# Six store tiles, weight loads on another queue, and K rows in a shared tile, in the first stage of a two-part kernel

## The chip, the cores and the metric

The kernel runs on one core of a Trainium2 chip. The metric is the device time of one execution in microseconds (us), lower is better. The kernels ran on the same chip beside runs of the kernel before.

## The reference

Two independent parts, whose outputs are put side by side. Part A is a long convolution (a Hyena-like block): a four-tap shift of `k`, a product with `v`, a convolution over 2048 steps by FFT, and a product with `q`. Part B is attention with a recurrent memory: 64 segments of 32 rows, each of which needs the memory rows that the segment before it produced.

```python
# part A, S = 2048, D = 1024
k_shift = sum(k_pad[:, t:t + S] * shift_k[:, 3 - t] for t in range(4))
kv = k_shift * v
y  = irfft(rfft(kv, 2 * S) * rfft(ssm_k, 2 * S))[:S] + kv * ssm_D
a  = q * y
# part B, 64 segments, 8 memory rows, 32 heads of 128
for s in range(64):
    h = concatenate([mem, x[:, 32 * s:32 * s + 32]])
    q, k, v = (einsum('btd,dhe->bhte', h, W) for W in (Wq, Wk, Wv))
    p = softmax(where(mask, q @ k.T * scale, -1e9))
    o = einsum('bhte,hed->btd', p @ v, Wo)
    mem = o[:, :8]; outs.append(o[:, 8:])
return concatenate([a, b], axis=-1)      # everything in bfloat16
```

## The kernel before

The work runs in this order: a prologue; stage 1 of the FFT over 16 units of rows (this is what the change edits); a dense projection with the first K weights (tiles `kb_ps`), whose start I call the **hand-over**; the later FFT stages with more projections; and then the attention loop of 64 segments, which streams weights through a ring called `wring`. The parts that the change touches:

```python
X_LOAD, K_LOAD = 4, 0
...
k0pool = tc.tile_pool(name="a1_k0", bufs=4)              # row pairs of k, 4 KB each
wk     = tc.tile_pool(name="a1_wk", bufs=3)
ints   = slot16([128, 4096], I32, "ints")                # integers of the sine tables
shflat = slot16([1, 4096], BF, "shflat")                 # the taps; takes the OTHER 16 KB tile
nc.sync.dma_start(shflat[:], shift_k...)
...
def stage1(u_tile, t, scratch):
    sb = wk.tile([128, 2, 1024], BF, tag="s1_sb")         # three store tiles (bufs=3 of the pool)
    for h in range(2):
        pt = ps_big.tile([128, 1024], F32, tag="big")
        for hf in range(2):
            nc.tensor.matmul(pt[:, hf*512:(hf+1)*512], lhsT=F1h[h], rhs=u_tile[:, hf*512:(hf+1)*512])
        nc.scalar.copy(sb[:, h, :], pt[:])                # ScalarE empties PSUM
    return nc.sync.dma_start(scratch...[t], sb[:])        # 512 KB to DRAM

for t in range(16):
    ...                                                   # 8 transposes of ssm_k -> kt
    stage1(kt, t, SK1)
    if t % 2 == 0:
        K0 = k0pool.tile([128, 2048], BF, tag="K0")
        nc.sync.dma_start(K0[:], pair_rows(k, t))
        Vp = io.tile([128, 2048], BF, tag="Vt")           # two buffers
        nc.gpsimd.dma_start(Vp[:], pair_rows(v, t))
    u = wk.tile([128, 1024], BF, tag="u", bufs=2)
    ...                                                   # 8 products on VectorE (tile prod, bufs=8),
                                                          # summed on PE into ks_ps; u = ks_ps * Vt
    su_stores.append(stage1(u, t, SU1))
    if tables: tables.pop(0)()                            # sine tables for later stages
stage1_done(su_stores)

def stage1_done(su):
    make_consts(); make_xbt(su)                           # x rows, transposed: XBT (PE, then ScalarE)
    for kc in range(8):
        with tc.issue_after(su[K_LOAD + kc]):             # behind that store, on the sync queue
            group(0, 0, which=[kc], ws=ws)                # load a K weight into slot pw0..pw7;
    dense(0, 0, ws)                                       # if streamed later: also copy it to DRAM (WS), on GpSimd
```

`slot16` alternates between two 16 KB tiles, stage0 and stage1; `slot4` is here a function that alternates between two 4 KB slots (`pair`).

## Time and profile before

| | |
|---|---|
| three runs of the kernel before | 2158.19 us median (2157.98 to 2163.79) |
| span of its profile, mean granted clock of TensorE | 2160.2 us, 0.978 |
| hand-over | 117.75 us |
| first matmul of the attention loop | 429.0 us |
| end of the first and of the 64th segment | 462.2 and 2147.4 us |

I take the end of a segment from the start of ScalarE's last cast of that segment's output, and call the stretch between these two ends the loop. Two more things are needed later. First, the page's list of transfers, with the KB of one transfer and the median us from issue to landing, in the kernel before:

```profile
SK<-s_sb SPq DMA_DIRECT2D x16, 512.0 KB, 5.0
SU<-s_sb SPq DMA_DIRECT2D x16, 512.0 KB, 5.1
```

These are the stores out of the three tiles. Second, busy time by stretch in the loop (stretch, its length, then PE, PEld, DVE, ACT, POOL with counts, clock, DMA share, GB/s):

```profile
462.20:2147.38 1685.18, 1363.66 (x33447) 776.11 (x33451) 613.32 (x2205) 433.33 (x819) 295.59 (x938) 0.99 1.01 387
```

The DMA share of 1.01 suggests that its transfers bound the loop, at 387 GB/s; PE is busy for 1364 of 1685 us, and its longest wait there, 108.8 us in 258 pieces, is for `wring`. Nothing in the change is inside this stretch.

### The profile page before, as it was taken

What the parts mean: (1) busy time and instruction counts of PE and PEld (TensorE: products, weight loads), DVE (VectorE), ACT (ScalarE), POOL (GpSimd) and SP (SyncE); (2) the same over time, 40 slices, a digit from 0 to 9 for tenths busy, and PEclk for the clock granted to TensorE, in tenths of its full rate; (3) what the DMA queues carried; (4) which work ended last, traced back from release to release, by engine and by line L of the source; (5) the groups of instructions that cost most, each with busy time, mean ns of one, the idle gap of its engine ahead of it and who ended that gap; (6) DMA issues with size and microseconds to landing.
All of it is one profiled execution on the core that took longest, in us unless ns stands there. A gap on an engine that the chain in (4) does not pass through costs nothing. (4 is left out here: it accounts for less than half of the span.)

```text
span 2160.2 us, 81529 instructions
## 1 busy us (share of the span) xinstructions
PE 1745.9 (81%) x35731; PEld 939.3 (43%) x35764; DVE 866.7 (40%) x2735; ACT 638.5 (30%) x1131; POOL 426.5 (20%) x1100
## 2 busy tenths in 40 slices
PE   6887988978878877888888878888877888878886
PEld 3432333434444444444444444444444444444444
DVE  9726852133333333333333333333333333333332
ACT  6845521222222222222222222222222222222222
POOL 3013432201111111111112111111111111111111
PEclk9998999989999999999999999999999999999999
DMA  9888989999999999999999999999999999999996
GB/s 322 315 334 298 296 311 378 313 371 386 392 378 392 387 377 379 391 392 394 392 393 395 390 388 384 391 381 383 390 389 375 389 392 384 394 394 392 393 391 269
DMA packets 238311, 802.29 MB, mean 371 GB/s; under 512 B 34721, under 2 KB 34753, under 8 KB 237953
## 3 DMA queue, kind: packets, MB, share of 16 engines
q1 hardware_dynamic: 207186, 728.20, 88.0%
q0 software_dynamic: 25552, 58.39, 7.8%
q10 hardware_dynamic: 5216, 10.49, 1.3%
q8 instruction: 279, 4.57, 0.9%
q14 instruction: 78, 0.64, 0.1%
HBM read 737.56 MB, written 62.39 MB: 370 GB/s over the span
## 5 line engine op out<-in xcount | busy, mean ns | idle before, releaser
L920 PEld LDWEIGHTS <-rec 128*32 128x32 bf16 x12351 | 318.6, 96 | 470.9 <-issue 249.1
L920 PE MATMUL acc<-wring,rec 128*32 128x512 bf16 x3765 | 371.4, 384 | 132.4 <-DMA wring<-WS 114.9
L929 ACT CAST qkv_sb<-acc 128x512 bf16<-128x512 f32 x384 | 225.1, 586 | 650.1 <-PE acc L920 646.6
L1006 PEld LDWEIGHTS <-OT 128*32 128x32 bf16 x8192 | 220.2, 97 | 181.3 <-issue 153.6
L1006 PE MATMUL yacc<-wring,OT 128*32 128x256 bf16 x3072 | 156.6, 279 | 95.5 <-DMA wring<-WS 57.7
L920 PE MATMUL acc<-Wmid,rec 128*32 128x512 bf16 x3072 | 225.9, 384 | 0.0
L920 PE MATMUL acc<-Wres,rec 128*32 128x512 bf16 x2816 | 221.2, 380 | 0.0
L866 PEld LDWEIGHTS <-OTB 128*16 128x16 bf16 x4096 | 106.2, 90 | 101.3 <-issue 92.4
L992 ACT CAST OT<-OTp 128x512 bf16<-128x512 f32 x128 | 75.0, 586 | 241.7 <-PE OTp L984 241.7
L1022 DVE COPY KT<-tps 128x512 bf16<-128x512 bf16 x64 | 27.2, 425 | 295.3 <-PE tps L935 295.3
L993 DVE CAST OTB<-OTp 128x128 bf16<-128x128 f32 x128 | 37.4, 292 | 261.2 <-ACT OT L992 261.2
L821 POOL DMA_DIRECT2D rec<-REC x64 | 37.5, 586 | 520.9 <-issue 264.0
L768 DVE TENSOR_SCALAR wring<-OTp 128x384 int32<-128x384 int32 x126 | 112.3, 891 | 53.8 <-PE acc L920 45.7
L920 PE MATMUL acc<-pw,rec 128*32 128x512 bf16 x1544 | 131.1, 382 | 0.0
L896 POOL COPY KT<-rec 128x128 bf16<-128x128 bf16 x128 | 38.8, 303 | 419.8 <-PE SB L944 398.2
L881 POOL DMA_DIRECT2D out_dram<-YB x128 | 73.3, 580 | 242.2 <-DVE YB L879 221.8
L950 DVE TENSOR_REDUCE mx<-SB 128x5 f32<-128x200 f32 x128 | 47.1, 368 | 179.8 <-PE SB L944 179.8
L935 PEld LDWEIGHTS <-qkv_sb 128*128 128x128 bf16 x1024 | 62.9, 97 | 105.1 <-ACT qkv_sb L929 61.6
L866 PE MATMUL SB<-wring,OTB 128*16 128x256 bf16 x1488 | 79.6, 276 | 35.6 <-DVE SB L845 29.6
L935 PE MATMUL tps<-ident,qkv_sb 128*128 128x128 bf16 x1024 | 101.2, 221 | 8.0
L1006 PE MATMUL yacc<-Wlate,OT 128*32 128x256 bf16 x2048 | 105.3, 276 | 2.4 <-issue 1.7
L1062 ACT CAST Y<-yacc 128x256 bf16<-128x256 f32 x64 | 23.8, 372 | 243.8 <-PE yacc L1006 239.2
(231 smaller groups left out, 2688.4 us busy)
## 6 DMA issues: line engine op xcount, KB each, us to landing
wring<-WS SPq DMA_DIRECT2D x1215, 512.0 KB, 7.3
rec<-REC POOLq DMA_DIRECT2D x64, 192.0 KB, 6.1
SK<-s_sb SPq DMA_DIRECT2D x16, 512.0 KB, 5.0
SU<-s_sb SPq DMA_DIRECT2D x16, 512.0 KB, 5.1
Kg<-SK SPq DMA_DIRECT2D x32, 256.0 KB, 5.2
Ug<-SU SPq DMA_DIRECT2D x32, 256.0 KB, 5.8
REC<-stage POOLq DMA_DIRECT2D x16, 512.0 KB, 11.2
zt<-SZ SPq DMA_DIRECT2D x16, 512.0 KB, 7.6
```

The source lines that it names most:

```text
L768: nc.vector.tensor_scalar(out=dst, in0=src, scalar1=0, scalar2=None, op0=ALU.bitwise_or)
L821: nc.gpsimd.dma_start(rec[:], REC[:, s, :])
L866: nc.tensor.matmul(self.acc[32 * dq:32 * dq + W, x - o:y - o], lhsT=self.OTB[:, c, 4 * g + i, :], rhs=r, start=first and not self.seeded, ...
L881: nc.gpsimd.dma_start(bass.AP(outb.tensor, outb.offset + (SEG * NB * self.b + NX) * 2048 + 256 * dq, [[2048 * SEG, NB], [2048, 8], [1, 256 ...
L896: nc.gpsimd.tensor_copy(KT[:, :, :, 32:40], KBs[:, 128 * g:128 * g + 128].rearrange("p (c i t) -> p i c t", c=4, i=4))
L920: nc.tensor.matmul(self.acc[32 * c:32 * c + 32, x - 512 * c:y - 512 * c], lhsT=hT[:, kc, :], rhs=r, start=(kc == 0 and x == 512 * c), stop ...
L929: nc.scalar.copy(sb[:], self.acc[:])
L935: nc.tensor.transpose(tp[:, i * 128:(i + 1) * 128], sb[:, i * 128:(i + 1) * 128], ident[:])
L950: nc.vector.tensor_reduce(out=mx[:], in_=S, op=ALU.max, axis=AX.X)
L992: nc.scalar.copy(OT[:], o_view[:, :, :, 0:32])
L993: nc.vector.tensor_copy(OTB[:, :, 4 * g:4 * g + 4, 8 * j:8 * j + 8], o_view[:, :, :, 32:40])
L1006: nc.tensor.matmul(yacc[32 * dq:32 * dq + 32, x - o:y - o], lhsT=OT[:, c, i, :], rhs=r, start=(h == 0 and x == o), stop=(h == 31), tile_po ...
```

## The change

Its intent: ScalarE waits in stage 1 for one of three store tiles (8.5 us in the profile before). The row pairs of `k` move into a 16 KB tile that is otherwise idle, which frees room for six store tiles. For that tile to be free, the tap rows and the tables' scratch move into weight slots that are still empty. And the first K weights leave the sync queue, to be issued by GpSimd behind the `v` rows. The core of the diff (cut: the body and signature of `group`, the matmul that reads the tap rows, the handing on of the list `v_loads`, and the same edit in a second table function):

```diff
-X_LOAD, K_LOAD = 4, 0
+X_LOAD, K_LOAD = 4, 2
-        k0pool = c1.enter_context(tc.tile_pool(name="a1_k0", bufs=4, side="right"))
-        shflat = slot16([1, 4096], BF, "shflat")
-        nc.sync.dma_start(shflat[:], shift_k.rearrange("(o d) j -> o (d j)", o=1))
+        shflat = [slot4(i)[0:1, :] for i in (6, 7)]
+        for i in range(2):
+            nc.sync.dma_start(shflat[i], shift_k.rearrange("(o d) j -> o (d j)", o=1)[:, 2048 * i:2048 * i + 2048])
-            sines = slot4()[:, 0:32 * NP].rearrange("p (a b) -> p a b", b=32)
+            sines = slot4(4 + x)[:, 0:32 * NP].rearrange("p (a b) -> p a b", b=32)
-            sb = wk.tile([128, 2, 1024], BF, tag="s1_sb", name="s1_sb")
+            sb = wk.tile([128, 2, 1024], BF, tag="s1_sb", bufs=6, name="s1_sb")
+        kring = slot16([128, 4, 2048], BF, "K0")
-                K0 = k0pool.tile([128, 2048], BF, tag="K0", name="K0")
-                nc.sync.dma_start(K0[:], pair_rows(k, t))
+                K0 = kring[:, t // 2 % 4, :]
+                nc.sync.dma_start(K0, pair_rows(k, t))
-                nc.gpsimd.dma_start(Vp[:], pair_rows(v, t))
+                v_loads.append(nc.gpsimd.dma_start(Vp[:], pair_rows(v, t)))
-            u = wk.tile([128, 1024], BF, tag="u", bufs=2, name="u")
+            u = wk.tile([128, 1024], BF, tag="u", bufs=3, name="u")
-                    pr = wk.tile([128, 512], BF, tag="prod", bufs=8, name="prod")
+                    pr = wk.tile([128, 512], BF, tag="prod", bufs=10, name="prod")
-            with tc.issue_after(su[K_LOAD + kc].ins):
-                group(0, 0, which=[kc], ws=ws)
+            with tc.issue_after(vl[K_LOAD + kc // 2].ins):
+                group(0, 0, which=[kc], ws=ws, eng=nc.gpsimd)
-    run_a(ps0, pair, slot16, stage1_done, fill)
+    run_a(ps0, pw, slot16, stage1_done, fill)
```

More of the change, by code (lines that the diff above doesn't have):

```diff
@@ L171, in a_kernel @@
                 nc.tensor.matmul(pt[:, e * 512:(e + 1) * 512], lhsT=ones_row[0:1, :],
-                                 rhs=shflat[0:1, hf * 1024 + e * 512:hf * 1024 + (e + 1) * 512], start=True, stop=True)
+                                 rhs=shflat[hf // 2][:, hf % 2 * 1024 + e * 512:hf % 2 * 1024 + (e + 1) * 512], start=True, stop=True)
             nc.scalar.copy(SH[:, :, hf * 256:(hf + 1) * 256], pt[:].rearrange("p (d j) -> p j d", j=4))
@@ L214, in table_n @@
             nc.vector.tensor_scalar(out=aN, in0=aN, scalar1=4095, scalar2=None, op0=ALU.bitwise_and)
-            sines = slot4()[:, 0:64 * NS].rearrange("p (a b) -> p a b", b=64)
+            sines = slot4(4 + y)[:, 0:64 * NS].rearrange("p (a b) -> p a b", b=64)
             act_sin(sines, aN, 12)
@@ L237, in a_kernel @@
         nc.sync.dma_start(Kx[113:128], kx_src[112:127])
-        su_stores = []
+        su_stores, v_loads = [], []
+        kring = slot16([128, 4, 2048], BF, "K0")
         ktiles = {c: Kx[:, c + 3, :] for c in (-3, -2, -1)}
@@ L271, in a_kernel @@
                 tables.pop(0)()
-    stage1_done(su_stores)
+    stage1_done(su_stores, v_loads)
     def valid_re(k1):
@@ L491, in b_kernel, with stage1_done @@
     pools = {}
-    def stage1_done(su):
+    def stage1_done(su, vl):
         make_consts()
@@ L551, in b_kernel, with group @@
     copied, got = [], []
-    def group(m, g, temps={}, which=range(8), ws=None):
+    def group(m, g, temps={}, which=range(8), ws=None, eng=nc.sync):
         ws = ws or [None] * 8
@@ L557, in group @@
             if ch in res:
-                got.append(nc.sync.dma_start(res[ch], dram_chunk(ch)))
+                got.append(eng.dma_start(res[ch], dram_chunk(ch)))
                 ws[kc] = res[ch]
@@ L561, in group @@
                 t = temps[ch]() if ch in temps else pw()
-                got.append(nc.sync.dma_start(t[:], dram_chunk(ch)))
+                got.append(eng.dma_start(t[:], dram_chunk(ch)))
                 if ch in streamed:
```

## The prediction

What goes is the argument for two terms of 0 us, for the bandwidth that another issuer of the weights brings and for loads issued by GpSimd; of that, the medians of 6.7 and 5.8 us in the paragraph's last sentence remain ("that way" there means issued by GpSimd), and the rest was not shown when it was written. Between ScalarE and VectorE, the trace of before shows PE waiting for ScalarE's evacuations for 4.57, 1.68 and 1.05 us after the three late store waits; after the first of them PE ran its next sums for VectorE at 70.67 us, behind the matmul that had waited (69.87 us), and VectorE waited 4.87 us for these sums.

> **What bounds the kernel now.** The edits all lie in stage 1, the forward pass over `k` and `v` that runs while the attention weights start to arrive. I read the page first, to see how much of the time that stage is:
>
> ```profile
> DVE  9726852133333333333333333333333333333332
> ACT  6845521222222222222222222222222222222222
> DMA  9888989999999999999999999999999999999996
> ```
>
> One slice is 2160.2 / 40 = 54 us, so stage 1 is a little over the first two digits. From slice 9 on the DMA row is 9 throughout: that is the attention loop, whose 1215 transfers into `wring` the change does not touch. The chain of waits agrees: its largest entry is that transfer, and all of the 353 pieces it could follow lie after 1988 us, so for the early stage it is no guide. What the change can save is a shift of everything behind stage 1. Next I found where stage 1 hands over. PE's first projection matmul of the attention weights is the hand-over:
>
> ```profile
> 117.75 2.29 PE L606 MATMUL kb_ps<-XBT,pw 128*128 128x512 bf16 x5 [0.67 <-ACT XBT L548]
> ```
>
> Its weights had long landed; it waited for ScalarE's copies of the transposed x rows, which stand behind ScalarE's evacuations of stage 1. So the time at which ScalarE gets through its list sets the hand-over. I cut the stage where ScalarE first stops for long and asked for busy time by stretch (columns: PE, PEld, DVE, ACT, POOL with counts, then clock, DMA share, GB/s):
>
> ```profile
> 23.30:64.32 41.02, 33.81 (x167) 16.79 (x169) 40.52 (x94) 31.91 (x35) 5.01 (x9) 0.92 0.89 317
> 64.32:89.00 24.68, 18.39 (x90) 8.89 (x91) 17.67 (x45) 16.59 (x18) 1.59 (x3) 0.86 0.84 306
> 89.00:118.20 29.20, 22.35 (x119) 10.94 (x121) 15.88 (x50) 27.58 (x34) 0.79 (x3) 0.90 0.90 336
> ```
>
> The reader is to see two regimes. Until 64 us VectorE is busy 40.5 of 41.0 us (products, plus the four trigonometric tables): it is the bound, and ScalarE has 9 us of slack. After 64 us ScalarE is the bound: 16.6 + 27.6 = 44.2 us of work in 53.9 us, so it is idle for 9.7 us. DMA is near full throughout, which matters below. The waits of ScalarE and VectorE between 20 and 125 us, then the timeline of ScalarE, say what the idle time was:
>
> ```profile
> ACT s_sb L230 <- DMA SU<-s_sb: 5.6, 2, 4.5
> ACT s_sb L230 <- DMA SK<-s_sb: 2.9, 2, 1.6
> ```
> ```profile
> DVE u L268 <- PE ks_ps L265: 10.5, 6, 4.9
> ```
> ```profile
> 68.81 1.93 ACT L230 CAST s_sb<-s_ps 128x1024 bf16<-128x1024 f32 x2 [4.49 <-DMA SU<-s_sb]
> ...
> 73.05 1.01 ACT L230 CAST s_sb<-s_ps 128x1024 bf16<-128x1024 f32 x1 [1.08 <-PE ks_ps L265]
> ...
> 88.39 5.66 ACT L230 CAST s_sb<-s_ps 128x1024 bf16<-128x1024 f32 x6 [1.64 <-DMA SK<-s_sb]
> ...
> 103.57 5.59 ACT L230 CAST s_sb<-s_ps 128x1024 bf16<-128x1024 f32 x6 [1.28 <-DMA SK<-s_sb]
> ```
>
> A new evacuation into one of the three store tiles waited until an earlier store had landed. The store waits total 5.6 + 2.9 = 8.5 us. While ScalarE stands still, [...] VectorE starves: that is the 10.5 us in VectorE's row.
>
> [...] Here the `v` loads already go that way under a VectorE that is 99% busy, with 6.7 us from issue to landing at the median, against 5.8 us for the `k` loads of equal size on sync: no starvation of note, so I charge nothing.
>
> **The change part by part.**
>
> *K row pairs in the 16 KB tile.* Four slices of 4 KB replace four buffers of 4 KB: the same depth and the same reuse distance, so 0 us by itself. It frees 16 KB, which pays for three more store tiles (12 KB), one more `u` (2 KB) and two more products (2 KB).
>
> *Six store tiles.* Each store holds 512 KB and takes 5.0 us to land at the median, 9.0 at most; ScalarE makes a tile from two casts, and the row at 88.39 shows six casts in 5.66 us, so 1.9 us a tile. With three tiles ScalarE fills two others before it needs the first again, about 2 x 1.9 = 3.8 us after its store went out (an estimate), less than the landing. With six it fills five, 9.5 us, more than the worst landing seen. So all store waits should go. Before 64 us that is worth nothing: one such wait of 1.13 us ends at 40.84, inside the stretch that VectorE bounds. After 64 us, 4.49 + 1.64 + 1.28 = 7.4 us come straight off ScalarE's list. The pauses that followed the first of them (0.23, 1.08 and 0.65 us, PE and VectorE picking up again) sum to 2.0 us and should mostly go too. Gross: 9.4 us.
>
> *More `u` and product tiles.* They let VectorE run further ahead of PE. VectorE has 33.6 us of work in the 53.9 us after 64 us, so it does not bind there; 0 us.
>
> *Tap rows and table scratch in weight slots.* The tap load becomes two DMAs: one more issue of some 0.3 us on the sync queue, hidden behind the `ssm_k` loads. Slots 4 to 7 are needed for K weights only after the `v` loads of units 8 and 10, when the tables are done (last copies end near 51 us). 0 us.
>
> *First K weights on GpSimd behind v rows.* Before, they were issued on sync behind the stores; the first at 29.86 us, the last four late:
>
> ```profile
> 79.79 0.42 SPq L562 DMA_DIRECT2D pw<-in_B_Wk_dram  x1
> ...
> 94.43 1.23 SPq L562 DMA_DIRECT2D pw<-in_B_Wk_dram  x2
> ...
> 101.77 0.46 SPq L562 DMA_DIRECT2D pw<-in_B_Wk_dram  x1
> ```
> ```profile
> 31.69 0.55 POOL L255 DMA_DIRECT2D Vt<-in_A_v_dram  x1 [0.93 <-DVE u L268]
> ...
> 44.25 0.54 POOL L255 DMA_DIRECT2D Vt<-in_A_v_dram  x1
> 57.25 0.54 POOL L255 DMA_DIRECT2D Vt<-in_A_v_dram  x1 [0.68 <-DVE u L268]
> 65.28 0.54 POOL L255 DMA_DIRECT2D Vt<-in_A_v_dram  x1 [7.50 <-DVE u L268]
> ```
>
> Afterwards they go two at a time behind these four `v` loads, so all are issued by about 66 us. Four transfers of 512 KB leave the stretch after 64 us; at the loop's 390 GB/s each takes 1.34 us of all engines, so 5.4 us, plus one copy back to DRAM (2.7 us, read and write). Stage 1 after 64 us then needs (24.68 x 0.84 + 29.20 x 0.90) - 8.1 = 47.0 - 8.1 = 38.9 us of DMA, where a ScalarE without waits would give 53.9 - 9.4 = 44.5 us. That fits. But the stretch before needs 41.02 x 0.89 = 36.5 us plus those 8.1 = 44.6 us, 3.6 us more than it has: a backlog that spills over the 64 us mark, delays stores there and the last two x loads at the end. Of it I charge two thirds, 2.4 us.
>
> *Sum.* 9.4 - 2.4 = 7.0 us earlier hand-over, from 117.8 to about 110.8 us. Behind it lie 28 us of projection on a full PE (19.7 of the 20 us from 120 us on) and then stages whose loads are released by that projection's end or by PE; I expect the shift to arrive whole. 2158.2 - 7.0 = 2151.2, rounded to 2151.
>
> **The rivals.** *DMA takes over.* Over the first 110 us DMA share is about 0.89 on the mean, so if all gaps were closed stage 1 could not get below some 106 us anyway, and the store waits may only turn into later waits for the x loads or `k` rows. For it: the row at 68.81 was a store stuck in a crowd (two x loads, a `v`, a `k`, a copy within 10 us of it). Against it: right after that crowd the share fell, 0.84 in 64 to 89 us, which says that the wait itself starved DMA. It would leave 0 to 3 us: 2155 to 2158. I give it 1 in 4.
>
> *The `v` rows wait behind weights.* Copies of streamed weights to DRAM stand in GpSimd's queue and wait for their load to land (22 us in three waits before); with the loads there as well, a `v` load can be held. Against it: a `v` load is issued about two units (8 us and more) ahead of its use, and no VectorE wait on `v` exists. It would cost up to 5 us: 2158 to 2163. 1 in 10.
>
> *More than the store waits.* If the lighter sync queue also brings stores and x loads home sooner and VectorE regains part of its 10.5 us, ScalarE reaches its floor of 64.3 + 44.2 = 108.5 us and early `Wmid` loads relieve the crowd near 170 us: 10 to 14 us, 2144 to 2148. 1 in 6.
>
> **Range and chances.** The middle case spans 5 to 9.5 us gained. With the rivals' tails, and runs of before that spread from 2157.98 to 2163.79, 2144.5 to 2157.5 should hold 8 in 10. Two per cent would be 43 us; stage 1 has only 9.7 us of idle time to give on its bounding engine, so faster by over 2% gets 0.01 and slower by over 2% gets 0.01, same 0.98.
>
> **What would show it.** Right: no ScalarE wait on a store of `s_sb` after 64 us; ScalarE's busy time from there to the hand-over unchanged near 44 us with under 3 us of idle; the first projection matmul at 109 to 112 us; all first K weights issued on GpSimd by about 70 us; VectorE still over 95% busy from 25 to 64 us; and the same distance as before from hand-over to the end. Wrong: ScalarE waits on PE instead (VectorE short of `k` or `v`), a hand-over near 117 us with DMA share at 1, or a shift at the hand-over that is gone by 400 us.

## The result, and the profile after

The kernel after took 2161.28 us (median of 4 runs, 2158.93 to 2162.91), the kernel before beside it 2160.99 us (4 runs, 2157.98 to 2163.82). The ratio is 1.0001 with a 95% interval of 0.998 to 1.0022: the same within 2%. The gain of 7.0 us did not come in these runs. Ratios here and below are the mean time of one kernel's runs over the mean of the other's of the same rounds, so they are not quite the ratio of the medians. The class was right; the predicted time was not, as 2161.28 lies 3.8 us above the top of the range.

The profile shows the early stage much as the prediction wanted it. PE's row of the hand-over in the timeline:

```profile
112.33 4.00 PE L607 MATMUL kb_ps<-XBT,pw 128*128 128x512 bf16 x10 [0.86 <-ACT XBT L549]
```

It is 5.4 us earlier than before. Busy time by stretch, same columns as above:

```profile
23.30:64.00 40.70, 33.24 (x161) 16.31 (x163) 39.96 (x93) 31.23 (x35) 8.96 (x16) 0.96 0.89 319
64.00:89.00 25.00, 21.89 (x107) 10.28 (x108) 20.29 (x51) 22.08 (x25) 3.40 (x8) 0.93 1.01 397
89.00:112.40 23.40, 17.07 (x111) 8.78 (x111) 13.99 (x46) 22.44 (x29) 0.00 (x0) 1.00 0.84 321
```

ScalarE's work from 64 us to the hand-over is 22.08 + 22.44 = 44.5 us, as before, now in 48.4 us. Three of the prediction's signs are missed by a little: that leaves 3.9 us of idle where it named under 3, the hand-over is past its 112, and one store wait is left after 64 us. In the middle row, from 64 to 89 us, the DMA share is 1.01, where it was 0.84 in the nearly equal stretch before. (A run below has the same share with ScalarE busy for all 25 us, so the share alone is not the cost.) ScalarE's and VectorE's waits between 20 and 125 us:

```profile
ACT s_sb L230 <- PE s_ps L228: 11.2, 6, 4.4
...
ACT s_sb L230 <- DMA SU<-s_sb: 0.5, 1, 0.5
```
```profile
DVE u L269 <- DMA Vt<-in_A_v_dram: 1.5, 1, 1.5
```

The store waits fell from 8.5 to 0.5 us in this profile; in the three later profiles of the full kernel after they are 2.1, 1.3 and 2.9 us. What did not exist before is VectorE's wait for `v`. GpSimd's timeline shows where it comes from, and the list of transfers shows what the fuller DMA goes with:

```profile
66.46 1.05 POOL L563 DMA_DIRECT2D pw<-in_B_Wk_dram  x2
78.85 0.54 POOL L565 DMA_DIRECT2D WS<-pw  x1 [11.34 <-DMA pw<-in_B_Wk_dram]
79.38 0.53 POOL L256 DMA_DIRECT2D Vt<-in_A_v_dram  x1
```
```profile
SK<-s_sb SPq DMA_DIRECT2D x16, 512.0 KB, 7.4
SU<-s_sb SPq DMA_DIRECT2D x16, 512.0 KB, 8.0
```

A copy of a weight to DRAM stood 11.34 us at the head of GpSimd's queue, waiting for the weight to land, and the `v` load of unit 12 stood behind it. And a store now takes 7.4 to 8.0 us to land.

The lead over the kernel before is 7.1 us at the loop's first matmul (421.9 against 429.0) and 6.4 us at the end of the first segment. But the loop itself takes longer:

```profile
455.83:2148.39 1692.56, 1369.27 (x33447) 779.97 (x33451) 613.00 (x2205) 433.32 (x820) 294.44 (x938) 0.99 1.01 386
```

It has the same number of instructions and the same work on each engine, to within 6 us on PE, but it is 7.4 us longer, and at its end the lead is gone (2148.4 against 2147.4). One profile is one run, though, and the runs of one kernel differ by more than this, as the controls below show.

So two questions went to the chip. What does each part of the change do to the hand-over? And does a shift of the hand-over arrive at the end, or is it absorbed, or given back in the loop by the change or by accident? The theories: (1) the shift arrives whole, and what hides it is scatter between runs; (2) a DMA-bound loop absorbs it; (3) the change carries something into the loop that makes it longer. The expectations call the first of these theory A and a loop that gives the shift back theory B; from the doubled tap matmul on, A is an accident of this one build and B that the change does it. Theory C is that nothing was won on the mean.

### The profile page after: what moved, and what is told of

It reads as the page before. It is cut to its first block, busy times and chain, and to the rows that moved or that the text cites. A ratio compares the mean times of both kernels' runs of the same rounds, so it can differ in the third digit from the quotient of the medians.

```text
span 2160.4 us, 81539 instructions
## 1 busy us (share of the span) xinstructions
PE 1748.1 (81%) x35731; PEld 941.1 (44%) x35764; DVE 867.7 (40%) x2735; ACT 637.9 (30%) x1131; POOL 429.9 (20%) x1108
## 3 DMA queue, kind: packets, MB, share of 16 engines
q8 instruction: 279, 4.57, 0.9%
## 5 line engine op out<-in xcount | busy, mean ns | idle before, releaser
L921 PE MATMUL acc<-wring,rec 128*32 128x512 bf16 x3765 | 376.7, 387 | 136.1 <-DMA wring<-WS 116.5
L769 DVE TENSOR_SCALAR wring<-OTp 128x384 int32<-128x384 int32 x126 | 112.3, 891 | 57.1 <-PE acc L921 49.0
```

Of the source, the lines that this page charges most:

```text
L769: nc.vector.tensor_scalar(out=dst, in0=src, scalar1=0, scalar2=None, op0=ALU.bitwise_or)
L921: nc.tensor.matmul(self.acc[32 * c:32 * c + 32, x - 512 * c:y - 512 * c], lhsT=hT[:, kc, :], rhs=r, start=(kc == 0 and x == 512 * c), stop ...
```

## The experiments

All had 5 rounds; all but the two shortened kernels give the reference's result.

**The loop cut to 8 segments: before and after.** Wrong results (56 segments are missing). The same edit in both kernels was meant to take out most of what scatters, and to leave the early stages (cut: the same edit in `last`).

```diff
+    N_RUN = 8
+    loads = [(s, ch) for s, ch in loads if s < N_RUN]
-        if 0 < s < n_seg:
+        if 0 < s < N_RUN:
-        for s in range(n_seg):
+        for s in range(N_RUN):
```

> The kernel before with the attention loop cut from 64 segments to 8 (wrong output on purpose: the later rows are not written). In the profile of the full kernel before, segment 0 ended at 462 us and segments 1 to 7 took 27 us each. Every theory expects about 462 + 7 x 27 + 15 = 670 us; the run is the base for the shortened changed kernel. If the loop is what makes full runs differ by up to 6 us from one another, these runs should lie within 1 to 2 us.

> The changed kernel with the loop cut to 8 segments in the same way. Theory A (the 5.4 us won at the hand-over reach the loop and stay; the full time hides them in the scatter of the loop) and theory B (the loop gives them back, by the end of its 64 segments) both expect 5 to 8 us under the shortened kernel before, as the lead in the two profiles was 6 to 9 us over segments 0 to 8. Theory C (the shorter stage 1 of the profiled execution was itself a lucky one, and nothing is won on the mean) expects a difference of under 2 us.

Measured: 663.27 us for before (4 runs, mean 662.5) and 659.75 us for after (5 runs, mean 659.6), 2.9 us less on the means. In their profiles the hand-over is at 117.02 and 113.34 us (3.7 us earlier), the end of the first segment at 463.35 and 457.52, and the end of the eighth at 649.74 and 645.95 us (3.8 us earlier). The runs still scatter by 5.3 and 9.7 us, where 1 to 2 were expected, so 2.9 us on nine runs is not clear of scatter, and the 5 to 8 us that A and B expected did not come. What follows, from one profile each: the stages between the hand-over and the loop do not absorb the shift; but it is nearer to 4 us than to the 5.4 of the first pair of profiles.

**Before and after once more, unchanged.** Controls.

> A control: the kernel before, unchanged, submitted as if it were a change. The ratio must be 1 within its interval; what matters is the scatter of its times and where its profile's segments end against the first profile of the same kernel. Theory A expects two profiles of the same kernel to drift apart by several us over the 64 segments in either direction (a loop of 1681 to 1693 us). Theory B expects the loop of the kernel before to take 1685 us again within 2 us.

> The changed kernel again, unchanged, over more rounds. Theory A expects the mean to be 4 to 7 us under the kernel before (ratio 0.997 to 0.998) once enough rounds are taken, with hand-over near 112 us and a loop between 1681 and 1693 us. Theory B expects a ratio of 1.000 within 0.001, hand-over near 112 us, and a loop 5 to 8 us longer than that of the kernel before, near 1692 us, each time.

Measured: 2161.05 us for before (6 runs; ratio 0.9985, interval 0.9964 to 1.0006) and 2156.74 us for after (6 runs from 2152.85 to 2174.85; ratio 0.998, 0.9948 to 1.0013), with 2165.39 us for the shared runs of before. What follows: one kernel scatters by up to 22 us from run to run, and a kernel against itself gives 0.9985. In the profiles the hand-over is at 117.48 and 112.64 us. The loop takes 1682.7 us in before and 1688.4 us in after.

**One store tile instead of six.** A large shift of the hand-over, to see whether any of it is absorbed later.

```diff
-            sb = wk.tile([128, 2, 1024], BF, tag="s1_sb", bufs=6, name="s1_sb")
+            sb = wk.tile([128, 2, 1024], BF, tag="s1_sb", bufs=1, name="s1_sb")
```

> A lever: the changed kernel with one store tile instead of six, so that each evacuation waits for the store before it and the hand-over comes much later (32 stores with about 5 us of landing each, of which perhaps 2 to 3 us were hidden: hand-over at about 180 to 220 us instead of 112). Theory A (a shift at the hand-over arrives at the end whole, and only the scatter of the loop hides small ones) expects total time to rise by the shift of the hand-over within 6 us, and a loop of 1682 to 1693 us. Theory B (the loop gives back what stage 1 does, whole or in part) expects the rise of the total to be smaller than the shift by a fraction that is plain at this size, a quarter or more, with a loop under 1670 us.

Measured: 2239.65 us, ratio 1.0344 (1.0309 to 1.0379). PE's row of the hand-over, and one of ScalarE's waits between 20 and 200 us:

```profile
174.44 1.67 PE L607 MATMUL kb_ps<-XBT,pw 128*128 128x512 bf16 x7 [1.50 <-ACT XBT L549]
```
```profile
ACT s_sb L230 <- DMA SK<-s_sb: 37.2, 10, 8.6
```

The first segment ends at 531.5 us, 71 us later than in before (the mean of 462.2 and 459.4), and the time is longer by 77 us on the means of the pooled runs (2240.1 against 2163.5). What follows: a shift of stage 1 is not absorbed by the loop, although its DMA share is 1.01. Theory (2) falls. But the shift does not arrive just as it was either, as theory A expected (within 6 us, with a loop of 1682 to 1693 us): it is 57 us at the hand-over (174.4 against 117.4 on the mean of before's three profiles), 71 at the first segment and 77 in the time, and the loop of this profile takes 1698.2 us. The trace lost 103 us to the lower clock, against 48 in before (both (1 - granted clock) x span, with a clock of 0.954 and 0.978).

**K weights back on the sync queue; three store tiles.** Two partial undoings of the change.

```diff
-X_LOAD, K_LOAD = 4, 2
+X_LOAD, K_LOAD = 4, 0
-    stage1_done(su_stores, v_loads)
+    stage1_done(su_stores, su_stores)
-            with tc.issue_after(vl[K_LOAD + kc // 2].ins):
-                group(0, 0, which=[kc], ws=ws, eng=nc.gpsimd)
+            with tc.issue_after(vl[K_LOAD + kc].ins):
+                group(0, 0, which=[kc], ws=ws)
```

> The changed kernel with the first K weights back on the sync queue behind the stores of units 0 to 7, as before; six store tiles and the rest kept. If the weights on GpSimd's queue cost something (the row wait of 1.5 us on v, the DMA share of 1.01 from 64 to 89 us), the hand-over comes 1 to 2 us earlier than 112.3 to 112.6 us; if they are what brought the gain, it goes back towards 117 us; if neither, it stays at 112 to 113 us. My own theory is the first or the last: 111 to 113 us.

```diff
-            sb = wk.tile([128, 2, 1024], BF, tag="s1_sb", bufs=6, name="s1_sb")
+            sb = wk.tile([128, 2, 1024], BF, tag="s1_sb", bufs=3, name="s1_sb")
```

> The changed kernel with three store tiles instead of six, all else kept. The theory that the store tiles bring the whole gain expects ScalarE's waits on stores to come back (7 to 9 us) and the hand-over at 117 to 119 us. The rival, that moving the weights and scratch brings it, expects 112 to 114 us.

Measured, weights on sync: 2150.15 us, ratio 0.9949 (0.9909 to 0.999). PE's hand-over row, ScalarE's timeline and the matching row of GpSimd's:

```profile
109.81 20.45 PE L607 MATMUL kb_ps<-XBT,pw 128*128 128x512 bf16 x86 [0.80 <-ACT XBT L549]
```
```profile
62.91 9.41 ACT L230 CAST s_sb<-s_ps 128x1024 bf16<-128x1024 f32 x10
...
108.19 2.05 ACT L549 COPY XBT<-xbt_ps 128x512 bf16<-128x512 bf16 x4 [1.55 <-PE xbt_ps L547]
```
```profile
73.47 0.53 POOL L256 DMA_DIRECT2D Vt<-in_A_v_dram  x1 [7.00 <-DVE u L269]
```

ScalarE works from 62.91 to about 106.6 us with one pause of 0.18 us, and then waits 1.55 us for the last `x` rows. The `v` load of unit 12 goes out at 73.47 us, 5.9 us earlier than in after, as soon as VectorE has freed its buffer. Busy time from 64 to 89 us:

```profile
64.00:89.00 25.00, 23.57 (x124) 11.49 (x125) 24.83 (x63) 25.00 (x29) 1.59 (x3) 1.00 1.02 406
```

The DMA share is as full as in after (1.02 against 1.01), yet ScalarE is busy for all 25.00 us, where after's four profiles have 20.0 to 23.7 us. So how full the DMA is does not tell the two apart; what it carries at that time does: in after the eight weights are all sent by 67 us, here the last four go out from 73 to 92 us. The worst landing of a store differs accordingly: 8.5 us here (of the 19 of 32 that the trace tells), 12.2 to 15.0 us in after.

Measured, three tiles with the weights on GpSimd: 2168.27 us, ratio 1.0004 (0.9969 to 1.0039), hand-over at 122.85 us, 5.4 us later than before. The longest wait in ScalarE's timeline:

```profile
72.22 1.93 ACT L230 CAST s_sb<-s_ps 128x1024 bf16<-128x1024 f32 x2 [5.96 <-DMA SU<-s_sb]
```

What follows: the store tiles bring the gain, and the move of the weights takes part of it back. With three tiles the store waits come to 9.9 + 4.4 = 14.3 us, against 8.5 in before, so the weights crowd the stores; with six tiles most of that is hidden. A store took 12.8 us at worst, also with three tiles.

**After, a third time.** A control.

> The changed kernel once more, for the mean and for another loop. Theory A: hand-over 112 to 113 us, total 3 to 7 us under the mean of the runs of the kernel before in this call, loop anywhere from 1681 to 1693 us. Theory B: total within 2 us of the kernel before, loop 1688 us or more.

Measured: 2164.01 us, ratio 0.9987 (0.9953 to 1.0021); hand-over at 114.44 us, the loop 1691.6 us. In this profile VectorE's wait for the late `v` load is longer than in the first; in the second and the fourth there is none:

```profile
90.79 0.69 DVE L269 TENSOR_TENSOR u<-ks_ps,Vt 128x512 bf16<-128x512 f32 x1 [4.30 <-DMA Vt<-in_A_v_dram]
```

**Weights on sync, again; the store tiles alone; the copies to DRAM issued late; after a fourth time.** For the size of the weights' part and for how it works. The store tiles alone are the kernel before with six store tiles and the K rows in the 16 KB tile, nothing else. In "copies late", the weights stay on GpSimd, but their copies to DRAM are issued behind the last `v` load, so that no `v` load stands behind a waiting copy (cut in its diff: the signature, and the branch for calls without `late`).

> Six store tiles with the K weights on the sync queue, unchanged from the earlier run of it, to confirm it as a better version. Hand-over 109 to 111 us again, ScalarE without a wait on a store after 64 us. In total I expect 6 to 10 us under the mean of the kernel before in this call (2154 to 2158 if the kernel before averages 2164), and a loop between 1678 and 1693 us, longer where the trace has more half-clock windows in it. If the earlier 10 us were luck of the loop, the mean lies within 5 us of the kernel before.

```diff
-        k0pool = c1.enter_context(tc.tile_pool(name="a1_k0", bufs=4, side="right"))
-            sb = wk.tile([128, 2, 1024], BF, tag="s1_sb", name="s1_sb")
+            sb = wk.tile([128, 2, 1024], BF, tag="s1_sb", bufs=6, name="s1_sb")
+        kring = slot16([128, 4, 2048], BF, "K0")
-                K0 = k0pool.tile([128, 2048], BF, tag="K0", name="K0")
-                nc.sync.dma_start(K0[:], pair_rows(k, t))
+                K0 = kring[:, t // 2 % 4, :]
+                nc.sync.dma_start(K0, pair_rows(k, t))
```

> The kernel before with only two of the edits: k row pairs in the 16 KB tile and six store tiles. Tap rows, table scratch, products, u and K weights as before. If the store tiles are all that helps, hand-over 109 to 111 us as with the rest of the edits, and 5 to 9 us off the total on the mean. If the third u and the two more products matter, the hand-over is later by 1 us or more than 109.8.

```diff
-                group(0, 0, which=[kc], ws=ws, eng=nc.gpsimd)
+                group(0, 0, which=[kc], ws=ws, eng=nc.gpsimd, late=vl[-1].ins)
-                    copied.append(nc.gpsimd.dma_start(stream_src(ch), t[:]))
+                    with tc.issue_after(late):
+                        copied.append(nc.gpsimd.dma_start(stream_src(ch), t[:]))
```

> The changed kernel, but the four copies of K weights to DRAM are issued on GpSimd only after the last v load, so that no v load stands behind a copy that waits for its weights to land. Theory Q (order in GpSimd's queue delays the v rows) expects the v load of unit 12 issued near 73 us instead of 79 to 81, no VectorE wait on v, hand-over 110 to 111 us. Theory R ([...] stores land later, up to 12 us, and six tiles run out) expects store waits and a hand-over still at 112 us or later.

> The changed kernel again. Hand-over 112 to 114.5 us. If its loop is longer than that of the kernel before as such, the loop takes 1688 us or more a fourth time; if the loop's length is chance, a value under 1688 us is as likely as one above. In either case I expect the time of each single run to follow its granted clock (each 0.001 less clock goes with 1.5 us more).

Measured, weights on sync: 2154.25 us, ratio 0.9969 (0.9945 to 0.9992), hand-over at 109.44 us: the first result repeats. Its loop of 1679.6 us lost 5.2 us to the lower clock, where the first run's of 1684.4 us lost 12.0.

Measured, store tiles alone: 2157.7 us, ratio 0.9982 (0.9958 to 1.0005), hand-over at 112.99 us. This is 3.4 us later than with the tap rows and the scratch moved as well and the third `u` and two more products (the mean of 109.81 and 109.44), although no wait for a store or for PE longer than 0.24 us is left after 42 us. The cause is in the beginning of the stage: ScalarE's timeline, and the wait of the sync queue between 5 and 45 us,

```profile
39.64 1.93 ACT L229 CAST s_sb<-s_ps 128x1024 bf16<-128x1024 f32 x2 [10.27 <-PE s_ps L227]
```
```profile
SPq L252 <- ACT pair L108: 9.0, 1, 9.0
```

The sync queue waited 9.0 us before it could load `k` rows, for ScalarE's sines of the tables. Without the tap edit, the alternation of the two 16 KB tiles gives the K rows the tile that holds the tables' integers, and all four tables had to be made before the first `k` row could land; it was issued at 29.43 us, where with the tap edit it goes out at 8.96. So this run is not a clean test of the tiles alone. It shows something else: the tap rows' move is what makes the 16 KB tile free.

Measured, copies late: 2154.5 us, ratio 0.9962 (0.9943 to 0.9982); hand-over at 112.04 us. GpSimd's timeline:

```profile
73.29 0.53 POOL L256 DMA_DIRECT2D Vt<-in_A_v_dram  x1 [5.95 <-DMA Vt<-in_A_v_dram]
...
83.28 2.11 POOL L569 DMA_DIRECT2D WS<-pw  x4
```

The `v` load is early again, VectorE no longer waits for it, and yet the hand-over is no earlier than in after: now ScalarE waits 1.7 us for a store. So the queue's order is visible, but not what limits: taking it away alone gains nothing at the hand-over. What is left is that the weights go out early, among the stores: those issued between 60 and 79 us land after 9.6 to 12.6 us here, after at most 8.3 us with the weights on sync. That this sets the hand-over is argued and not tested: no run sent the weights later on GpSimd's queue, which would part their time from their queue.

After, the fourth time: 2161.38 us, ratio 0.9991 (0.9969 to 1.0012), hand-over 113.14, loop 1694.2 us. Over the runs of all full-length kernels the time goes with the clock by 1.3 us for each 0.001 (0.60 us for each us lost, from the scatter below, in 2160 us), where 1.5 was expected. Here VectorE does not wait for `v`, and ScalarE waits for a store instead:

```profile
ACT s_sb L230 <- DMA SU<-s_sb: 2.9, 1, 2.9
```

By then the four profiles of after had loops of 1688.4 to 1694.2 us and all other builds 1678.2 to 1685.2 us but for the one with one tile (1698.2), although the edits leave the loop's code alone and its counts of instructions are the same. Theory (3) was alive. The rest of the runs are on this.

**A tap matmul twice; three idle memsets; the weights' move alone; copies late again.** The first two change nothing but the place of instructions in a program. The third is the kernel before with only the move of the weights (cut in its diff: the changes to `group` and the handing on of `v_loads`).

```diff
-            for e in range(2):
+            for e in ((0, 0, 1) if hf == 3 else (0, 1)):
```

> The kernel after with one matmul of the tap broadcast done twice, before stage 1: the same result, the same loop, every later PE instruction one place further on in the program. The four profiles of the kernel after have an attention loop (end of the first segment to end of the last) of 1688 to 1694 us, against 1678 to 1685 us in all other builds, though the loop's own instructions are the same. Theory A [...]: hand-over 112 to 115 us as in the kernel after, but a loop of 1686 us or less, and a mean time of about 2154, ratio 0.994 to 0.997. Theory B (the order of the weights, the store tiles or the freed pool does it, by whatever way): loop of 1688 us or more, ratio 0.997 to 1.002.

```diff
             nc.gpsimd.memset(M[:], 0.0)
+        for i in range(3):
+            nc.gpsimd.memset(Mre[0:1, 0, 0:1], 0.0)
```

> The kernel after with three memsets of one element on GpSimd in the prologue, where GpSimd is idle: the same result; only GpSimd's program and its first microsecond move. Theory A (accident of this one build): a loop of 1686 us or less is as likely as not, mean time 2154 to 2160; Theory B (carried in by the change): loop of 1688 us or more, ratio 0.997 to 1.002. If this one is long and the run with the doubled matmul is short, the place of PE's instructions matters; if both are short, it is chance from build to build.

```diff
-X_LOAD, K_LOAD = 4, 0
+X_LOAD, K_LOAD = 4, 2
-                nc.gpsimd.dma_start(Vp[:], pair_rows(v, t))
+                v_loads.append(nc.gpsimd.dma_start(Vp[:], pair_rows(v, t)))
-            with tc.issue_after(su[K_LOAD + kc].ins):
-                group(0, 0, which=[kc], ws=ws)
+            with tc.issue_after(vl[K_LOAD + kc // 2].ins):
+                group(0, 0, which=[kc], ws=ws, eng=nc.gpsimd)
```

> The kernel before with one part of the change alone: the first K weights issued on GpSimd behind the v loads of units 4 to 10 (three store tiles, K rows in four buffers, two u, eight products, as before). My reading of the earlier runs (weights on GpSimd cost 2.5 to 5 us, by holding back the v load of unit 12 and by crowding the stores): hand-over 120 to 124 us, mean 3 to 6 us over the kernel before, ratio 1.001 to 1.003. The prediction's step (a backlog of 2.4 us, no hold of v rows): hand-over 119 to 121 us, ratio 1.001. The rival that the freed sync queue helps: hand-over at or under 117 us, ratio below 1. The loop: theory B in the form that the weights' order lengthens it says 1688 us or more; theory A says under 1686 us.

> The kernel after with the copies of the first K weights back to DRAM issued behind the last v load, a second time. The first time: hand-over 112.0 us, loop 1685.2 us, ratio 0.9962, while the kernel after in the same call had 0.9991 and 1694.2 us. Theory A (the loop's length belongs to the build[...]): again 1686 us or less, ratio 0.995 to 0.998. If instead the loop's length is chance from profile to profile: anywhere in 1680 to 1694 us.

Measured: the doubled matmul 2163.93 us, ratio 0.9989 (0.9963 to 1.0016), hand-over 113.29, loop 1695.2 us: long, against theory A of the text above. The three memsets 2157.33 us, ratio 0.9964 (0.994 to 0.9988), hand-over 114.75, and a short loop:

```profile
458.78:2144.60 1685.82, 1365.28 (x33447) 775.75 (x33450) 612.69 (x2205) 433.32 (x820) 295.07 (x938) 0.99 1.01 387
```

Copies late again: 2156.77 us, ratio 0.9962 (0.9937 to 0.9986), hand-over 112.32, loop 1685.6 us: a repeat of 1685.2.

The weights' move alone: 2166.62 us, ratio 1.0009 (0.9983 to 1.0036), loop 1684.7 us. Its hand-over is later than I expected, 7.9 us behind the mean of before's three profiles; PE's row, ScalarE's longest wait and GpSimd's:

```profile
125.35 1.44 PE L606 MATMUL kb_ps<-XBT,pw 128*128 128x512 bf16 x3 [0.67 <-ACT XBT L548]
```
```profile
73.86 1.93 ACT L230 CAST s_sb<-s_ps 128x1024 bf16<-128x1024 f32 x2 [7.42 <-DMA SU<-s_sb]
```
```profile
80.41 0.54 POOL L564 DMA_DIRECT2D WS<-pw  x1 [11.44 <-DMA pw<-in_B_Wk_dram]
```

The wait that was 4.49 us in before is 7.42 us: a store stuck behind the weights that GpSimd sent out between 60 and 69 us. With the old three tiles the move of the weights is a plain loss at the hand-over. Its time does not show it beyond scatter (1.3 us on the means, interval up to 7.8 us), and its loop is short in the one profile taken, so nothing here shows that the weights' move by itself lengthens the loop.

**Three memsets again; one memset.**

> The three idle memsets on GpSimd a second time. The first time the attention loop took 1685.8 us, the hand-over was at 114.75 us and the ratio 0.9964, against 1688 to 1694 us and 0.998 to 1.000 for the kernel after. If the length of the loop belongs to a build (theory A): again 1686 us or less, ratio 0.995 to 0.998. If it is chance from profile to profile: anywhere from 1680 to 1695 us.

```diff
             nc.gpsimd.memset(M[:], 0.0)
+        for i in range(1):
+            nc.gpsimd.memset(Mre[0:1, 0, 0:1], 0.0)
```

> The kernel after with one idle memset of one element on GpSimd instead of three. Theory A, in the form that any neutral shift draws the loop's length anew: 1680 to 1695 us, no favourite, ratio 0.995 to 1.000. Theory B (the change lengthens the loop): 1688 us or more, ratio 0.998 to 1.001; together with a repeat of a short loop under three memsets that would leave B as a tendency and not as a rule.

Measured: 2160.22 us, ratio 0.9977 (0.9957 to 0.9997), loop 1686.2 us; and 2158.46 us, ratio 0.998 (0.9953 to 1.0006), loop 1688.9 us, between the two groups.

**All together.** Hand-over and loop are from one profile for each label, in us; several labels of one kernel are listed in order. "Clock lost" is (1 - granted clock) summed over the loop, in us; "run" is how far the profiled run's time lay from the mean of all runs of its kernel, in us.

| kernel | hand-over | loop | clock lost | run | ratio to before |
|---|---|---|---|---|---|
| before | 117.75, 117.48 (short: 117.02) | 1685.2, 1682.7 | 14.4, 12.3 | -0.7, -6.0 | control 0.9985 |
| after | 112.33, 112.64, 114.44, 113.14 (short: 113.34) | 1692.6, 1688.4, 1691.6, 1694.2 | 24.6, 15.4, 23.9, 18.8 | 2.0, -3.4, 4.5, 4.9 | 1.0001, 0.998, 0.9987, 0.9991 |
| after, a tap matmul twice | 113.29 | 1695.2 | 22.3 | 1.9 | 0.9989 |
| after, three memsets | 114.75, 112.50 | 1685.8, 1686.2 | 17.1, 18.4 | 0.0, -3.5 | 0.9964, 0.9977 |
| after, one memset | 112.67 | 1688.9 | 17.1 | -3.0 | 0.998 |
| after, copies late | 112.04, 112.32 | 1685.2, 1685.6 | 12.2, 9.7 | -0.3, -1.8 | 0.9962, 0.9962 |
| after, weights on sync | 109.81, 109.44 | 1684.4, 1679.6 | 12.0, 5.2 | -3.3, -6.8 | 0.9949, 0.9969 |
| after, three store tiles | 122.85 | 1678.2 | 5.1 | -9.4 | 1.0004 |
| after, one store tile | 174.44 | 1698.2 | 32.4 | 4.2 | 1.0344 |
| before, six tiles and K ring | 112.99 | 1681.2 | 13.6 | -8.2 | 0.9982 |
| before, weights on GpSimd | 125.35 | 1684.7 | 8.5 | -3.0 | 1.0009 |

Two things in this table bear on theory (3). The loops compare single runs, and the runs that were profiled are not typical: those of after lay 2.0 us above the mean of their kernel, those of before 3.4 us below it, and those of three other builds 5 to 9 us below. Of the 7.7 us by which after's loops are longer than before's (1691.7 against 1684.0), up to 5.4 us is thus the luck of which run was profiled. And over the 18 profiles the loop's length follows the clock lost in it: correlation 0.90, 0.70 us for each us lost (0.86 and 0.72 without the one tile). Which of the two brings the other is not shown.

**The scatter.** The 65 runs of before have a mean of 2163.5 us and a standard deviation of 5.2 us, and go from 2147.65 to 2177.81 us. More than half of their variance follows the granted clock (correlation 0.76 among the 61 with a clock on record, so 57%; a correlation, not a cause shown): over the timed runs of all full-length kernels, each set against the mean of its own kernel, a run is 0.60 us longer (standard error 0.05) for each us of clock that it lost, where the clock lost is (1 - granted clock) x span, some 47 us in a run of before. At that rate the lost clock of a run of before would be worth some 28 us (an estimate from these two numbers, if the correlation is a cause). The traces of before and after show what the clock did: it has two values only, full and 0.5, and in the loop it falls to 0.5 for 3.41 us at a time, once in each trace for three times that. In the 3.4 us before each of these stretches PE was busy for 0.34 to 0.56 of the time, against 0.81 over the loop; what makes the clock fall is not shown. Between the first segment's end and the 64th's lie 8 to 14 stretches at half clock in the four profiles of after, and 8 and 6 in the two of before.

## Why the prediction was wrong

In short: what bounds stage 1, and what releases it, was right. Two terms of the sum failed. The starting point was 2158.2 us, the median of three runs, where 65 runs have a mean of 2163.5. And the weights were charged 2.4 us, where they cost 3.6, because six tiles were measured against the worst landing of the old traffic (9.0 us), while with the weights sent early among the stores the worst was 12.2 us and more.

The pooled runs split the miss. After's 22 runs have a mean of 2160.9 us, 9.9 us over the predicted 2151.0. Of this, 5.3 us are the starting point (2163.5 - 2158.2), 0.2 us is the rounding of 2151.2, 2.8 us are gain that did not come at the hand-over (7.0 - 4.2, below), and 1.6 us are what separates 4.2 from the 2.6 us gained in time (2163.5 - 2160.9). The standard error of that 2.6 is 1.3 us, so the last part is not clear of scatter. Step by step:

- **The bound of stage 1, and its release.** Right. ScalarE sets the hand-over, its work stayed at 44 us, and the store waits after 64 us went from 7.4 to 0.5 us in the first profile and to 1.1 us on the mean of the eight of after and its neutral variants; with the weights on sync none is left. The experiments with one and three tiles move the hand-over the way this step says.
- **Gross gain of 9.4 us.** Nearly right. With the weights on sync, ScalarE goes from its row at 62.91 us to a hand-over at 109.81, in 46.9 us, where before it took from 62.30 to 117.75, 55.45 us: 8.5 us are saved. The part that is missing is that ScalarE now arrives before the last `x` rows and waits 1.55 us for them, a wait that the old store waits had hidden. On the means of the hand-overs the gross gain is 7.8 us (117.4 - 109.6).
- **Nothing for the tap rows and the scratch.** Not refuted as a cost. ScalarE reaches its row near 62 us 0.6 us later in the first profile of after than in that of before (62.93 against 62.30), but the same row starts at 62.30, 62.53 and 64.46 us in before's three profiles, so 0.6 us is not resolved. Their worth was missed: with six tiles and the K ring alone, the hand-over is 3.4 us later, as the `k` rows then wait 9.0 us for the tables.
- **The weights' 2.4 us.** The mechanism is the one named, the size too small. Against the version with weights on sync (109.6 on the mean) the eight profiles of after and its three neutral variants have a mean hand-over of 113.2: 3.6 us. With three tiles the same move costs more: 7.9 us on top of before. The assumption that six tiles cover the worst landing failed with it: it took 9.0 us as the worst, from the kernel before, while the slowest store in each profile of after took 12.2 to 15.0 us, longer than the head start of 9.5 us, so that store waits of 0.5 to 2.9 us stayed. It is the weights that did this and not the six tiles: with six tiles and the weights on sync the slowest store took 8.5 and 8.4 us, with three tiles and the weights on GpSimd 12.8 and 12.6. (More stores in flight lengthen the median, to 6.0 to 8.1 us in the builds with six tiles and the weights on sync.) The last two `x` loads, which the prediction also saw delayed, were not: they landed after 3.6 and 4.5 us in after, after 5.0 us each in before.
- **The rival of `v` rows behind weights**, which got 1 in 10, came true as an order: the `v` load was held 5.9 us, and VectorE waited for it 1.5 to 4.3 us in four of the eight profiles, and not at all in the other four. It did not decide: with the copies out of the way the hand-over stayed at 112.
- **The rival that DMA takes over**, 1 in 4, did not come in the form given: the share did go to 1.01 and 1.02 from 64 to 89 us, but with it the version with weights on sync still kept 7.8 us at the hand-over.
- **Net hand-over.** 7.0 us predicted; 4.2 us measured (117.4 on the mean of three profiles, to 113.2 on eight). At the loop's first matmul the lead was 5.6 us (428.9 on the mean of before's three profiles, 423.3 on the same eight).
- **"I expect the shift to arrive whole."** Nothing absorbs it: 71 us at the first segment became 77 us in the time with one tile, and the 7.8 us of the version with weights on sync became 8.9 us (mean ratio 0.9959, of 2163.5). For the kernel after it stays open. The mean of its four ratios is 0.9990, 2.2 us, and with the neutral variants that of eight is 0.9984, 3.5 us, against 5.6 us at the loop's first matmul. Its loop was longer in each of its four profiles, and the eight profiles of its family all lie above the nine of the other builds, leaving out the one with one tile, if only by 0.2 us. But the runs profiled in these eight lay 0.4 us above the means of their kernels, and those of the nine 4.4 us below, so 4.8 of the 7.4 us between the two groups may be no more than the choice of runs. Nor do the memsets settle it: three of them went with loops of 1686.0 us (mean of two) instead of 1691.7 (mean of four), but the times differ by 2.5 us with a standard error of 1.5, one memset gave 1688.9 and a doubled matmul 1695.2, and four profiles of after alone differ by 5.8 us. What the long loops do have in common is more half clock: 15 to 25 us lost in each of the eight, 5 to 14 in each of the nine. That something of the change lengthens the loop, by some 2 or 3 us on these means, is neither shown nor ruled out.
- **The starting point and the range.** This is the term that failed most. The range took before's spread from three runs, 2157.98 to 2163.79, and centred on their median. Of 65 runs the mean is 5.3 us higher, and single runs go from 2148 to 2178. A range of 13 us, placed by three of them, was too narrow for an absolute time. The prediction had put the hand-over at 109 to 112 us and the class at "same"; what it could honestly say of the time was a difference, not a place.

The version with weights on sync beats both kernels: 2153.9 us on the mean of 12 runs, against 2160.9 (after) and 2163.5 (before), with both of its intervals below 1. It is the change without its last part.

## What to carry to other kernels

When a wait is removed by more buffers, the landing time that they must cover is that of the new traffic, not of the old: take the worst landing (9.0 us in before, 12.2 to 15.0 us in after), and ask what the freed engine will send into the same transfers. A load that is moved "behind" another in a queue also stands before the next one, together with every waiting copy that follows it: here a copy that waited 11.34 us held a `v` load for 5.9 us. And before predicting a time within a few us, take the scatter from many runs and predict the difference; before comparing parts of two profiles, look where in that scatter the profiled runs lie; an event in the trace, such as the hand-over here (117.0 to 117.8 us in before's three profiles, 112.3 to 114.4 in after's five), resolves a part of the change that the total time, with a standard deviation of 5.2 us, cannot.
